# Moving LN apply and the phi clamps to the vector engine, transposing all of x first, and giving the projections two PSUM banks

## The chip, the cores and the metric

The kernel runs on one core of a Trainium2 chip. The metric is the time of one launch in device microseconds. Five engines work side by side, each with its own fixed queue of instructions: PE (matmuls), ACT (activations), DVE (vector), POOL (the general-purpose engine) and SP, which issues DMAs. Results of PE lie in eight PSUM banks of 512 float32 columns each. DVE and ACT read them; POOL does not in this kernel.

## The reference, cut to what matters

One x of 2048 tokens by 448 channels goes through two branches that a gate mixes:

```
g = sigmoid((x * gate_w).sum(-1))
a = A(x)                      # 16 heads of 28, 4 segments of 512 tokens
b = B(x)                      # token-mixing MLP, 2048 -> 1792 -> 2048
out = g * a + (1 - g) * b

A: q, k, v = x @ wq, x @ wk, x @ wv
   phi(t) = where(t > 0, t + 1, exp(t))
   per segment s, M and z starting from 0:
     a_dot = softmax(q k^T * scale + causal mask) v
     a_mem = (phi(q) M) / (phi(q) z + 1e-6)
     o = sigmoid(beta) * a_mem + (1 - sigmoid(beta)) * a_dot
     M += phi(k)^T v ;  z += sum(phi(k))
   return o @ wo
B: h = layernorm(x) over channels
   u = gelu(w1^T h + b1) ; y = w2^T u + b2      # contraction over tokens
```

## The kernel before, in words

**Tiles.** x is held in `xh` as 16 tiles of 128 tokens by 448 channels. `transposes(tc)` (L461 to L485) turns the four tiles of token chunk tc into `xT`: two groups ("halves") of eight 128-column PE transposes (L471), each group into one PSUM bank, and one copy-out per group (L484 on DVE; the very first, L481, on ACT). For each chunk, `do_k` (L499) and `do_q` (L520) make four projection tiles each through `proj_d` (four matmuls of 512 columns, L491); k is copied out by ACT (L503), q by DVE (L524). `do_v` (L539) makes one tile per 128 tokens (four matmuls of 449 columns, L545; the last column is the gate), copied out by ACT (L551, and L554 for the gate's tanh).

**phi.** `do_kphi` (L506) and `do_qphi` (L527) compute phi as max(t, 0) + min(exp(t), 1): the exponential on ACT (L509, L530), the clamp (L511, L532), and one DVE instruction that adds the max (L513, L535). phi of k is then transposed by a DMA that SP issues (L516) from one of two `kphi` buffers. `do_mst(s)` (L557) multiplies the transposed phi(k) of segment s with v (16 matmuls, L564), adds to the running float32 state (L574, L577) and writes the scaled state `mst_sb` (L579).

**Attention.** There are 16 units of one segment and four heads, in order of segment. `scores` (L664) makes three blocks per unit in banks 0 to 3 (L675), takes one exponential over four banks (L684, ACT), and masks the diagonal 128 columns on POOL (L688). `pv_unit` (L692) multiplies with v into bank 4 (L711) and, from unit 4 on, makes the product with the memory state in bank 5 (L697). DVE transposes both (L724, L725), divides (L733 to L736), POOL adds them (L738) and DVE transposes back (L744). `wo_tile` (L750) multiplies a finished 128-token tile with wo (L757) and gates it on ACT (L763); it uses bank 5 too, and for the last tiles banks 0 to 2.

**MLP.** LN needs statistics of each tile (L623, L625, DVE), then four small instructions on POOL for all tiles together (`ln_coef`, L628: L632 to L636, of which L633 is a power), then `ln_apply` (L638), one tensor-scalar with two per-partition scalars per tile, in place on `xh`. `mm1` (L769) makes each of the 14 tiles of u from 16 matmuls of 448 columns, one per token tile (L774), then GELU with three ACT and two DVE instructions (L778 to L789). `mm2` (L793) makes each of 16 output tiles from 14 matmuls (L799), one DVE instruction (L804) and a DMA out. `mlp_next` gives MLP tile i bank 6 + i % 2. Weights of both layers come in 15 loads of 256 columns (`ring_load`, L386) through seven slots, of which three have memory of their own; the fourth and fifth lie on `xT`, the sixth on the padded wq and wk, the seventh on the transposed phi(k), and each of these can be loaded once its first owner is done.

**What sets the order.** Every instruction is declared to a planner (`Sched`, L49) with an engine, the tiles it reads and writes, an estimated cost and a priority. Dependences follow the order of declaration: who writes a bank waits for all who were declared earlier on that bank. `plan` (L113) then plays a greedy list schedule with these costs and freezes each engine's order; on the chip each engine runs its list strictly in order. Lower priority numbers go first: copies-out and small work 0, attention 100 plus the unit, projections, phi and LN around 200, wo 300, MLP1 400, MLP2 500. A DMA is one more such instruction on the queue that issues it.

**Banks.** `next_bank` (L440) hands out `banks_now` (L438) in rotation: all eight for the first chunk, then banks 5, 6, 7 (L828). The rotation counts transposes, projection tiles and the state product alike. In iteration tc of the loop at L830 the order of declaration is transposes(tc), k, q and v of tc, the gate columns, `do_mst(tc - 1)`, then phi of q and k. All of this is declared before attention and MLP. `fn_warm` (L444) runs matmuls on zeros at the start, before x has landed.

Of the kernel before, what the change touches and what calls it, by code (L numbers as in the profile page):

```python
# [5 lines left out]
ACT = mybir.ActivationFunctionType  # L6
ALU = mybir.AluOpType
# [34 lines left out]


ENGINES = ("PE", "ACT", "DVE", "POOL", "SP")
HOP = 70.0
SWITCH = 110.0


class Sched:  # L49
# [11 lines left out]
    def op(self, eng, fn, reads=(), writes=(), name=None, dma=False, out=False, cost=100.0, lat=None, prio=None,  # L61
           mode=None, nbytes=0):
        o = Op()
        o.eng, o.fn, o.name, o.idx = eng, fn, name, len(self.ops)
        o.is_event, o.ev_val, o.knowledge, o.waits = False, None, None, None
        o.cost = cost
        o.lat = (170.0 if eng == "PE" else 0.0) if lat is None else lat
        o.prio = (self.now if prio is None else prio, o.idx)
        o.mode = mode
        o.nbytes = nbytes  # L70
        o.start = o.end = o.pos = None
        if dma:
# [24 lines left out]
        for r in writes:  # L97
            w = r.last_write
            if w is not None:
                (after if r.psum and eng == "PE" and w.evspace == "PE" else need)(w)  # L100
            for rd in r.reads:
                (after if r.psum and eng == "PE" and rd.evspace == "PE" else need)(rd)
        o.deps = list(deps.values())
        o.order = list(order.values())
        for r in reads:
            r.reads.append(o)
        for r in writes:
            r.last_write = o
            r.reads = []
        self.ops.append(o)  # L110
        return o
# [119 lines left out]


def act_cost(n, sbuf=False, ptr=0):
    return n / 1.2 + (115.0 if sbuf else 75.0) + 90.0 * ptr


def dve_cost(n, rate=1.0):
# [1 line left out]


def pool_cost(n):
    return n / 1.2 + 200.0


def build_kernel(nc, X, WQ, WK, WV, WO, BETA, W1, B1, W2, B2, GW, OUT):
# [108 lines left out]

    xv = x2.rearrange("(t p) d -> p t d", p=128)

    def load_x(t0, n):
        op("SP", lambda e: e.dma_start(xh[:, t0 : t0 + n, :], xv[:, t0 : t0 + n, :]),
           writes=R_x[t0 : t0 + n], name=f"ldx{t0}", dma=True, cost=500, nbytes=n * 128 * 896)
# [9 lines left out]
    load_x(4, 4)  # L369
    load_x(8, 4)  # L370
    load_x(12, 4)
# [71 lines left out]

    def fn_warm(e):  # L444
        last = None
        for _ in range(9):
            last = e.matmul(bank(7)[:, 0:512], warm[:, 0:128], warm[:, 0:512], start=True, stop=True,  # L447
                            skip_group_check=True)
# [12 lines left out]
    def transposes(tc):  # L461
        for half in range(2):
            b = next_bank()
            tb = bank(b).bitcast(BF16)

            def fn(e, half=half, tb=tb):
                last = None
                for ti in range(4):
                    for c2 in range(2):
                        c = half * 2 + c2  # L470
                        last = e.matmul(tb[0:CK, c2 * 512 + ti * 128 : c2 * 512 + ti * 128 + 128],  # L471
                                        xh[:, 4 * tc + ti, c * CK : c * CK + CK], ident[:, :], is_transpose=True,
                                        start=True, stop=True, skip_group_check=True)
                return last

            op("PE", fn, reads=R_x[4 * tc : 4 * tc + 4] + [R_ident], writes=[R_bank[b]], name=f"trx{tc}_{half}",
               mode="f", cost=8 * 66, prio=P_PROJ + tc - (50 if tc else 0))
            dst = xT[0:CK, 2 * half : 2 * half + 2, tc * 512 : tc * 512 + 512]
            src = tb[0:CK, :].rearrange("p (c t) -> p c t", c=2)
            if tc == 0 and half == 0:  # L480
                op("ACT", lambda e, dst=dst, src=src: e.activation(dst, src, ACT.Copy), reads=[R_bank[b]],  # L481
                   writes=[R_xT[tc][half]], name=f"xTcp{tc}_{half}", cost=act_cost(1024), prio=P_BASE)
            else:
                op("DVE", lambda e, dst=dst, src=src: e.tensor_copy(dst, src), reads=[R_bank[b]],  # L484
                   writes=[R_xT[tc][half]], name=f"xTcp{tc}_{half}", cost=dve_cost(1024), prio=P_PROJ + tc - 150)  # L485

    def proj_d(w_pad, R_w, hg, tc, b):
        def fn(e):
# [17 lines left out]
    def do_kphi(tc, hg):  # L506
# [1 line left out]
        ks = kT[:, hg, tc * 512 : tc * 512 + 512]  # L508
        op("ACT", lambda e: e.activation(kphi[:, p, :], ks, ACT.Exp), reads=[R_kT[hg][tc]],  # L509
           writes=[R_kphi[p]], name=f"ek{tc}_{hg}", cost=act_cost(512, True), prio=P_PROJ + tc)  # L510
        op("POOL", lambda e: e.tensor_scalar(kphi[:, p, :], kphi[:, p, :], 1.0, 0.0, op0=ALU.min, op1=ALU.max),  # L511
           reads=[R_kphi[p]], writes=[R_kphi[p]], name=f"mk{tc}_{hg}", cost=pool_cost(512), prio=P_PROJ + tc)
        op("DVE", lambda e: e.scalar_tensor_tensor(kphi[:, p, :], ks, 0.0, kphi[:, p, :], op0=ALU.max, op1=ALU.add),  # L513
           reads=[R_kT[hg][tc], R_kphi[p]], writes=[R_kphi[p]], name=f"phk{tc}_{hg}", cost=dve_cost(512),
           prio=P_PROJ + tc)
# [11 lines left out]
    def do_qphi(tc, hg):  # L527
# [1 line left out]
        ph = phq[:, hg, (tc - 1) * 512 : tc * 512]  # L529
        op("ACT", lambda e: e.activation(ph, qs, ACT.Exp), reads=[R_qT[hg][tc]],  # L530
           writes=[R_phq[hg][tc]], name=f"eq{tc}_{hg}", cost=act_cost(512, True), prio=P_PROJ + tc)
        op("POOL", lambda e: e.tensor_scalar(ph, ph, 1.0, 0.0, op0=ALU.min, op1=ALU.max),  # L532
           reads=[R_phq[hg][tc]], writes=[R_phq[hg][tc]], name=f"mq{tc}_{hg}", cost=pool_cost(512),
           prio=P_PROJ + tc)
        op("DVE", lambda e: e.scalar_tensor_tensor(ph, qs, 0.0, ph, op0=ALU.max, op1=ALU.add),  # L535
           reads=[R_qT[hg][tc], R_phq[hg][tc]], writes=[R_phq[hg][tc]], name=f"phq{tc}_{hg}", cost=dve_cost(512),
# [99 lines left out]
        po(lambda e: e.tensor_tensor(nmr[:], vpe[:], rstd[:], op=ALU.mult), [R_vpe, R_rstd], [R_nmr], "nmr")  # L636

    def ln_apply(t):  # L638
        op("POOL", lambda e: e.tensor_scalar(xh[:, t, :], xh[:, t, :], rstd[:, t : t + 1], nmr[:, t : t + 1],  # L639
                                             op0=ALU.mult, op1=ALU.add),  # L640
           reads=[R_x[t], R_rstd, R_nmr], writes=[R_x[t]], name=f"ln{t}", cost=580, prio=P_PROJ - 10)

    def gate_cols(s):
        t4 = slice(4 * s, 4 * s + 4)
# [19 lines left out]
    def scores(n):  # L664
# [21 lines left out]
        for c0 in (0, 384) if f == 1 else (0,):  # L686
            d = pv[:, :, c0 : c0 + 128]
            op("POOL", lambda e, d=d: e.affine_select(d, d, pattern=[[0, 4], [1, 128]], compare_op=ALU.is_ge,  # L688
                                                      fill=0.0, base=0, channel_multiplier=-1),
               reads=[R_P[u % 2][f]], writes=[R_P[u % 2][f]], name=f"mask{n}_{c0}", cost=740, prio=pr)  # L690

    def pv_unit(u):  # L692
        s, hg = unit(u)
# [38 lines left out]
        if s > 0:  # L732
# [3 lines left out]
            dv(lambda e: e.tensor_tensor(t3[1], t3[1], rb[1], op=ALU.mult), [R_tt[tb][1], R_rec[tb]], [R_tt[tb][1]],  # L736
               "om", 650)
            op("POOL", lambda e: e.tensor_tensor(o, t2[:, 0, :], t2[:, 1, :], op=ALU.add), reads=R_tt[tb],  # L738
               writes=[R_ob[tb]], name=f"o{u}", cost=1350, prio=pr)
# [4 lines left out]
        dv(lambda e: e.transpose(oT[:, hg, s * 512 : s * 512 + 512], o), [R_ob[tb]], [R_qT[hg][s]], "ot", 500)  # L744

    def ag(T):
        s, g = divmod(T, 4)
# [174 lines left out]
```

## Time and profile before

| | |
|---|---|
| three runs | 222.96, 223.94, 226.82 us (median 223.94) |
| the profiled execution | 224.56 us, span from first to last instruction 222.8 us |
| mean granted PE clock over the span | 0.954 |
| first scores matmul | 21.05 us |
| first exponential of attention (L684) | 21.64 us |
| first MLP1 matmul (L774) | 85.7 us |
| first MLP2 matmul of the final run (L799) | 177.56 us |
| HBM read and written | 18.13 MB and 1.84 MB |

How to read it: the page gives each engine's busy time over the span; the span in 40 slices, with the clock that PE was granted; the chain of work that ended last, followed back from the last instruction; and groups of equal instructions by line, engine and shape, with busy time, count, mean in ns, and the idle time before them with what ended it. A matmul's row shows its latency, so a back-to-back run is better read from its start and end: 224 matmuls of L799 take 42.39 us. Some matmul records are missing from a trace.

### The profile page before, as it was taken

The page shows a single profiled execution, that of the slowest core. Times are in us where ns is not written, and L with a number is a line of the kernel's source. Part 1 is how long each engine was busy: PE and PEld are TensorE (multiplying, and loading weights), DVE is VectorE, ACT ScalarE, POOL GpSimd, SP SyncE. Part 2 cuts the span into 40 slices and gives each one's busy share as a digit, 9 for nine tenths or more (in the row PEclk, how much of TensorE's full clock was granted, in tenths as well). Part 3 has the DMA queues.
Part 4 walks back from the last instruction along what each step waited for, and adds up shares of the span by engine and source line. Part 5 has one row for each costly group of instructions (what it writes and reads, how often), then busy time and mean ns, then how long its engine had stood idle before and what let it go on. Part 6 is the DMA issues. An engine that isn't in the chain of part 4 may idle for free.

```text
span 222.8 us, 3401 instructions
## 1 busy us (share of the span) xinstructions
PE 194.6 (87%) x1343; PEld 86.7 (39%) x1350; DVE 145.3 (65%) x261; ACT 138.1 (62%) x181; POOL 105.8 (47%) x133
## 2 busy tenths in 40 slices
PE   7599696968866988958879898999999999999994
PEld 2434342423432324312334343434444555555552
DVE  1759895549994497998997957866868142222222
ACT  2264999676995699936999878999975610000000
POOL 8120419999999567966484445455452000000000
PEclk9999999679996799985999999999999999999999
DMA  5999802000101201139640744352355067111111
GB/s 125 297 272 288 206 0 47 4 1 19 29 3 24 47 4 23 24 71 302 175 93 3 188 134 119 79 165 73 95 166 165 3 185 206 41 55 51 41 41 41
DMA packets 42451, 21.75 MB, mean 98 GB/s; under 512 B 7876, under 2 KB 42436, under 8 KB 42436
## 3 DMA queue, kind: packets, MB, share of 16 engines
q1 hardware_dynamic: 41304, 21.13, 35.7%
q10 hardware_dynamic: 1132, 0.41, 1.0%
q8 instruction: 10, 0.16, 0.3%
q14 instruction: 5, 0.04, 0.1%
HBM read 18.13 MB, written 1.84 MB: 90 GB/s over the span
## 4 chain that ended last, share of the span: by engine, by line
PE 52%; DVE 17%; POOL 16%; ACT 12%; issue 2%
PE t L799 19%; PE t L774 11%; PE t L491 7%; ACT t L684 6%; POOL t L639 6%; POOL t L688 5%; PE t L757 4%; PE t L545 3%; PE t L711 2%; DVE t L734 2%; DVE t L736 2%; DVE t L784 2%; PE t L675 2%; PE t L447 2%; DVE t L744 2%
## 5 line engine op out<-in xcount | busy, mean ns | idle before, releaser
L684 ACT ACTIVATE t<-t 128x2048 bf16<-128x2048 f32 (+1 forms) x48 | 77.2, 1608 | 5.4 <-PE t L675 5.3
L688 POOL TENSOR_SCALAR_AFFINE_SELECT t<-t 128x512 bf16<-128x512 bf16 x64 | 47.5, 747 | 39.2 <-ACT t L684 38.1
L774 PE MATMUL t<-t 128*128 128x448 bf16 x224 | 50.6, 359 | 2.4 <-ACT t L781 1.3
L799 PE MATMUL t<-t 128*128 128x448 bf16 x224 | 42.5, 352 | 0.0
L491 PE MATMUL t<-t 112*128 112x512 bf16 x128 | 35.8, 425 | 4.2 <-DVE t L484 2.1
L774 PEld LDWEIGHTS t<-t 128*128 128x128 bf16 x224 | 20.7, 99 | 24.2 <-issue 7.2
L804 DVE SCALAR_TENSOR_TENSOR t<-t 128x448 bf16<-128x448 f32 x16 | 10.9, 684 | 29.0 <-PE t L799 29.0
L799 PEld LDWEIGHTS t<-t 128*128 128x128 bf16 x224 | 21.9, 98 | 20.5 <-DVE t L789 0.2
L738 POOL TENSOR_TENSOR t<-t 128x512 bf16<-128x512 f32 x12 | 16.8, 1401 | 13.3 <-DVE t L736 13.3
L675 PE MATMUL t<-t 28*128 28x512 bf16 (+3 forms) x256 | 17.8, 312 | 5.8 <-ACT t L684 5.7
L491 PEld LDWEIGHTS t<-t 112*128 112x128 bf16 x128 | 12.2, 106 | 21.8 <-issue 6.8
L725 DVE STREAM_TRANSPOSE t<-t 128x512 f32<-128x512 f32 x16 | 11.3, 709 | 11.4 <-PE t L711 11.2
L711 PE MATMUL t<-t 128*32 128x512 bf16 (+3 forms) x256 | 12.7, 322 | 6.9 <-POOL t L688 6.8
L545 PE MATMUL t<-t 112*128 112x449 bf16 x64 | 15.9, 385 | 1.5 <-DVE t L524 1.3
L757 PE MATMUL t<-t 128*128 128x448 bf16 x64 | 15.1, 368 | 1.5 <-DVE t L744 1.3
L784 DVE SCALAR_TENSOR_TENSOR t<-t 128x448 f32<-128x448 f32 x14 | 10.7, 766 | 7.1 <-ACT t L781 6.8
L503 ACT ACTIVATE t<-t 128x512 bf16<-128x512 f32 x16 | 9.6, 605 | 8.9 <-PE t L491 8.9
L639 POOL TENSOR_SCALAR t<-t 128x448 bf16<-128x448 bf16 x16 | 14.7, 927 | 0.5 <-PE t L471 0.5
L744 DVE STREAM_TRANSPOSE t<-t 128x512 bf16<-128x512 bf16 x16 | 11.2, 703 | 4.7 <-POOL t L738 4.6
L675 PEld LDWEIGHTS t<-t 28*128 28x128 bf16 x256 | 5.2, 92 | 22.9 <-ACT t L684 16.3
L511 POOL TENSOR_SCALAR t<-t 128x512 bf16<-128x512 bf16 x12 | 9.2, 768 | 8.1 <-ACT t L509 8.1
L524 DVE CAST t<-t 128x512 bf16<-128x512 f32 x16 | 10.8, 680 | 3.4 <-PE t L491 3.1
(75 smaller groups left out, 230.9 us busy)
## 6 DMA issues: line engine op xcount, KB each, us to landing
t<-in_B_w_dram SPq DMA_DIRECT2D x7, 1024.0 KB, 6.2
t<-in_B_w_dram SPq DMA_DIRECT2D x8, 896.0 KB, 5.2
out_dram<-t SPq DMA_DIRECT2D x16, 112.0 KB, 1.7
t<-in_A_x_dram SPq DMA_DIRECT2D x3, 448.0 KB, 9.0
t<-in_A_x_dram SPq DMA_DIRECT2D x2, 224.0 KB, 5.0
t<-in_A_wk_dram ACTq DMA_DIRECT2D x1, 392.0 KB, 4.5
t<-in_A_wq_dram SPq DMA_DIRECT2D x1, 392.0 KB, 6.8
t<-in_A_wv_dram SPq DMA_DIRECT2D x1, 392.0 KB, 7.8
```

What stands on the lines that cost most here:

```text
L491: last = e.matmul(bank(b)[:, 0:512], w_pad[0:CK, c, hg * 128 : hg * 128 + 128], xT[0:CK, c, tc * 512 : tc * 512 + 512], start=(c == 0), st ...
L545: last = e.matmul(bank(b)[:, 0 : D + 1], xT[0:CK, c, t * 128 : t * 128 + 128], wvx[0:CK, c, :], start=(c == 0), stop=(c == NCT - 1), skip_ ...
L639: op("POOL", lambda e: e.tensor_scalar(xh[:, t, :], xh[:, t, :], rstd[:, t : t + 1], nmr[:, t : t + 1], op0=ALU.mult, op1=ALU.add), reads= ...
L675: last = e.matmul(bank(hl)[:, c0 : c0 + w_], kT[r, hg, s * 512 + j * 128 : s * 512 + j * 128 + 128], qT[r, hg, s * 512 + 128 * j : s * 512 ...
L684: op("ACT", lambda e: e.activation(pv, ps[:, 0:4, 0:w], ACT.Exp, scale=SCALE), reads=R_bank[0:4], writes=[R_P[u % 2][f]], name=f"exp{n}", ...
L688: op("POOL", lambda e, d=d: e.affine_select(d, d, pattern=[[0, 4], [1, 128]], compare_op=ALU.is_ge, fill=0.0, base=0, channel_multiplier=- ...
L711: last = e.matmul(bank(CTX)[32 * hl : 32 * hl + 32, 128 * j : 512], vaug[:, 4 * s + j, 32 * h : 32 * h + 32], pv[:, hl, c0 : c0 + w_], sta ...
L738: op("POOL", lambda e: e.tensor_tensor(o, t2[:, 0, :], t2[:, 1, :], op=ALU.add), reads=R_tt[tb], writes=[R_ob[tb]], name=f"o{u}", cost=135 ...
L744: dv(lambda e: e.transpose(oT[:, hg, s * 512 : s * 512 + 512], o), [R_ob[tb]], [R_qT[hg][s]], "ot", 500)
L757: last = e.matmul(bank(b)[:, 0:D], oT[:, hg, T * 128 : T * 128 + 128], wo_sb[:, hg, :], start=(hg == 0), stop=(hg == NHG - 1), skip_group_ ...
L774: op("PE", lambda e, st=st: e.matmul(bank(b)[:, 0:D], w1c[:, st, f2 * 128 : f2 * 128 + 128], xh[:, st, :], start=(st == 0), stop=(st == NT ...
L799: op("PE", lambda e, ft=ft: e.matmul(bank(b)[:, 0:D], w2c[:, ft, t2_ * 128 : t2_ * 128 + 128], uT[:, ft, :], start=(ft == 0), stop=(ft == ...
```

## The change

- `ln_apply` goes from POOL to DVE, the clamps of phi too (as a min with 1 alone, in place of a min and a max with 0).
- The transposes of chunks 1, 2 and 3 are declared among the v tiles of chunk 0, on the eight-bank rotation, at priority 200. `ln_coef` and `ln_apply` are declared right after the statistics.
- The later projections and state products rotate over banks 5 and 6; MLP1 tiles 0 to 3 all use bank 7, and later tiles alternate as before (tile 4 on 6, tile 5 on 7).
- `do_mst(s)` is declared one iteration later, after the projections of chunk s + 2, and the last one after the loop.
- The warm-up has 18 matmuls in place of 9.
- Tiles 2 and 3 of x are loaded from ACT's queue, wk from SP's queue behind tiles 0 and 1.
- Constants of the planner's cost model are changed: the hop between engines (70 to 80 ns), a delay behind ACT of 95 ns, slightly other costs of ACT, POOL, masks and transposes.

```
-HOP = 70.0
+HOP = 80.0
...
-        o.lat = (170.0 if eng == "PE" else 0.0) if lat is None else lat
+        o.lat = {"PE": 180.0, "ACT": 95.0}.get(eng, 0.0) if lat is None else lat
...
-    load_x(0, 2)
-    load_x(2, 2)
-    op("ACT", lambda e: e.dma_start(wk_nat[0:CK], WK.rearrange("(c p) d -> p c d", p=CK)), writes=R_P[0],
+    load_x("SP", 0, 2)
+    load_x("ACT", 2, 2)
+    op("SP", lambda e: e.dma_start(wk_nat[0:CK], WK.rearrange("(c p) d -> p c d", p=CK)), writes=R_P[0],
...
-        for _ in range(9):
+        for _ in range(18):
             last = e.matmul(bank(7)[:, 0:512], warm[:, 0:128], warm[:, 0:512], start=True, stop=True,
...
-               mode="f", cost=8 * 66, prio=P_PROJ + tc - (50 if tc else 0))
+               mode="f", cost=8 * 66, prio=P_PROJ)
...
-        op("POOL", lambda e: e.tensor_scalar(kphi[:, p, :], kphi[:, p, :], 1.0, 0.0, op0=ALU.min, op1=ALU.max),
-           reads=[R_kphi[p]], writes=[R_kphi[p]], name=f"mk{tc}_{hg}", cost=pool_cost(512), prio=P_PROJ + tc)
+        op("DVE", lambda e: e.tensor_scalar_min(kphi[:, p, :], kphi[:, p, :], 1.0),
+           reads=[R_kphi[p]], writes=[R_kphi[p]], name=f"mk{tc}_{hg}", cost=dve_cost(512, 4), prio=P_PROJ + tc)
...
-        op("POOL", lambda e: e.tensor_scalar(ph, ph, 1.0, 0.0, op0=ALU.min, op1=ALU.max),
-           reads=[R_phq[hg][tc]], writes=[R_phq[hg][tc]], name=f"mq{tc}_{hg}", cost=pool_cost(512),
+        op("DVE", lambda e: e.tensor_scalar_min(ph, ph, 1.0),
+           reads=[R_phq[hg][tc]], writes=[R_phq[hg][tc]], name=f"mq{tc}_{hg}", cost=dve_cost(512, 4),
...
-        op("POOL", lambda e: e.tensor_scalar(xh[:, t, :], xh[:, t, :], rstd[:, t : t + 1], nmr[:, t : t + 1],
-                                             op0=ALU.mult, op1=ALU.add),
-           reads=[R_x[t], R_rstd, R_nmr], writes=[R_x[t]], name=f"ln{t}", cost=580, prio=P_PROJ - 10)
+        op("DVE", lambda e: e.tensor_scalar(xh[:, t, :], xh[:, t, :], rstd[:, t : t + 1], nmr[:, t : t + 1],
+                                            op0=ALU.mult, op1=ALU.add),
+           reads=[R_x[t], R_rstd, R_nmr], writes=[R_x[t]], name=f"ln{t}", cost=dve_cost(448, 4), prio=P_PROJ - 10)
...
     do_small()
+    transposes(1)
     for t in range(4):
         do_v(t)
+        if t == 1:
+            transposes(2)
+    transposes(3)
     for t in range(NT):
         ln_stats(t)
+    ln_coef()
+    for t in range(NT):
+        ln_apply(t)
     load_wo()
...
-    banks_now[0] = [5, 6, 7]
+    banks_now[0] = [5, 6]
     gate_cols(0)
     for tc in (1, 2, 3):
-        transposes(tc)
...
         gate_cols(tc)
-        do_mst(tc - 1)
+        if tc > 1:
+            do_mst(tc - 2)
         for hg in range(NHG):
             do_qphi(tc, hg)
             if tc < 3:
                 do_kphi(tc, hg)
-    ln_coef()
-    for t in range(NT):
-        ln_apply(t)
+    do_mst(2)
     for _ in range(4):
         ring_load()
+    NB7 = 4
...
-        f_(a, 6 + i % 2)
+        f_(a, 7 if i < NB7 else 6 + i % 2)
```

More of the change, by code (lines that the diff above doesn't have):

```diff
@@ L233, in act_cost @@
 def act_cost(n, sbuf=False, ptr=0):
-    return n / 1.2 + (115.0 if sbuf else 75.0) + 90.0 * ptr
+    return n / 1.2 + (100.0 if sbuf else 80.0) + 90.0 * ptr
 def dve_cost(n, rate=1.0):
@@ L241, in pool_cost @@
 def pool_cost(n):
-    return n / 1.2 + 200.0
+    return n / 1.2 + 320.0
 def build_kernel(nc, X, WQ, WK, WV, WO, BETA, W1, B1, W2, B2, GW, OUT):
@@ L355, in build_kernel, with load_x @@
     xv = x2.rearrange("(t p) d -> p t d", p=128)
-    def load_x(t0, n):
-        op("SP", lambda e: e.dma_start(xh[:, t0 : t0 + n, :], xv[:, t0 : t0 + n, :]),
+    def load_x(eng, t0, n):
+        op(eng, lambda e: e.dma_start(xh[:, t0 : t0 + n, :], xv[:, t0 : t0 + n, :]),
            writes=R_x[t0 : t0 + n], name=f"ldx{t0}", dma=True, cost=500, nbytes=n * 128 * 896)
-    load_x(0, 2)
-    load_x(2, 2)
-    op("ACT", lambda e: e.dma_start(wk_nat[0:CK], WK.rearrange("(c p) d -> p c d", p=CK)), writes=R_P[0],
+    load_x("SP", 0, 2)
+    load_x("ACT", 2, 2)
+    op("SP", lambda e: e.dma_start(wk_nat[0:CK], WK.rearrange("(c p) d -> p c d", p=CK)), writes=R_P[0],
        name="ldwk", dma=True, cost=500, nbytes=401408)
@@ L368, in build_kernel @@
        name="ldwv", dma=True, cost=500, nbytes=401408)
-    load_x(4, 4)
-    load_x(8, 4)
-    load_x(12, 4)
+    for t0 in (4, 8, 12):
+        load_x("SP", t0, 4)
     op("ACT", lambda e: e.dma_start(wvx[0:CK, :, D : D + 1], GW.rearrange("(c p o) -> p c o", p=CK, o=1),
@@ L484, in transposes @@
                 op("DVE", lambda e, dst=dst, src=src: e.tensor_copy(dst, src), reads=[R_bank[b]],
-                   writes=[R_xT[tc][half]], name=f"xTcp{tc}_{half}", cost=dve_cost(1024), prio=P_PROJ + tc - 150)
+                   writes=[R_xT[tc][half]], name=f"xTcp{tc}_{half}", cost=dve_cost(1024, 2), prio=P_PROJ + tc - 150)
     def proj_d(w_pad, R_w, hg, tc, b):
@@ L689, in scores @@
                                                       fill=0.0, base=0, channel_multiplier=-1),
-               reads=[R_P[u % 2][f]], writes=[R_P[u % 2][f]], name=f"mask{n}_{c0}", cost=740, prio=pr)
+               reads=[R_P[u % 2][f]], writes=[R_P[u % 2][f]], name=f"mask{n}_{c0}", cost=750, prio=pr)
     def pv_unit(u):
@@ L738, in pv_unit @@
             op("POOL", lambda e: e.tensor_tensor(o, t2[:, 0, :], t2[:, 1, :], op=ALU.add), reads=R_tt[tb],
-               writes=[R_ob[tb]], name=f"o{u}", cost=1350, prio=pr)
+               writes=[R_ob[tb]], name=f"o{u}", cost=1400, prio=pr)
         else:
@@ L743, in pv_unit @@
                [R_tt[tb][0], R_rec[tb], R_omcol], [R_ob[tb]], "oa", 650)
-        dv(lambda e: e.transpose(oT[:, hg, s * 512 : s * 512 + 512], o), [R_ob[tb]], [R_qT[hg][s]], "ot", 500)
+        dv(lambda e: e.transpose(oT[:, hg, s * 512 : s * 512 + 512], o), [R_ob[tb]], [R_qT[hg][s]], "ot", 700)
     def ag(T):
```

## The prediction

> **What bounds the kernel now.** I read the page first: engine totals, clock row, and the chain that ended last.
>
> ```profile
> PE 194.6 (87%) x1343; PEld 86.7 (39%) x1350; DVE 145.3 (65%) x261; ACT 138.1 (62%) x181; POOL 105.8 (47%) x133
> PEclk9999999679996799985999999999999999999999
> PE 52%; DVE 17%; POOL 16%; ACT 12%; issue 2%
> ```
>
> No engine is full over the span, and POOL, the least busy, owns 16% of the chain. So the stages have different limits. I cut the span where the chain changes hands: first scores (21.05), POOL's run (33.37 to 68.84), the first read of unit 4's memory product (84.87), the last projection's consumer (102.84), the first MLP2 matmul (177.56).
>
> ```profile
> core 0: us, PE busy (x) PEld busy (x) DVE busy (x) ACT busy (x) POOL busy (x), PEclk, DMA share, GB/s
> 0.00:21.05 21.05, 17.19 (x72) 7.52 (x73) 12.31 (x50) 7.27 (x13) 6.97 (x15) 1.00 0.97 243
> 21.05:33.37 12.32, 10.17 (x92) 4.72 (x92) 10.87 (x28) 11.55 (x14) 3.39 (x5) 1.00 0.50 122
> 33.37:68.84 35.47, 25.81 (x215) 11.09 (x214) 26.16 (x41) 28.10 (x40) 34.45 (x43) 0.89 0.10 20
> 68.84:84.87 16.03, 14.75 (x100) 5.33 (x101) 10.11 (x17) 12.28 (x19) 11.36 (x16) 0.81 0.13 26
> 84.87:102.84 17.97, 14.36 (x117) 6.26 (x119) 17.76 (x24) 14.14 (x19) 14.13 (x15) 0.89 0.30 74
> 102.84:177.56 74.72, 70.00 (x531) 30.05 (x534) 55.90 (x87) 63.02 (x76) 35.51 (x42) 0.98 0.44 120
> 177.56:222.80 45.24, 42.37 (x224) 21.69 (x222) 12.20 (x18) 1.73 (x3) 0.00 (x0) 1.00 0.27 82
> 21.05:177.56 156.51, 135.08 (x1051) 57.45 (x1058) 120.80 (x194) 129.09 (x165) 98.84 (x118) 0.93 0.32 83
> ```
>
> The columns are the stretch, its length and each engine's busy time. From 33.37 POOL is busy 34.45 of 35.47 us while ACT has 28.10 and DVE 26.16. From 84.87 DVE is full (17.76 of 17.97). From 102.84 it is PE (70.00 of 74.72), and after 177.56 MLP2 alone. The pieces of the chain say what POOL was doing:
>
> ```profile
> 34.69 2.93 POOL t L633
> ...
> 39.40 3.22 POOL t L639 x4
> ...
> 43.21 2.79 POOL t L639 x4
> ...
> 51.27 1.60 POOL t L511 x2
> 52.87 2.17 POOL t L532 x3
> ...
> 64.75 3.45 POOL t L639
> ...
> 70.64 4.85 PE t L491 x12
> ...
> 177.56 42.39 PE t L799 x224
> ```
>
> LN apply (L639) and clamps (L511, L532) stand ahead of the masks and of the phi tiles. Behind those the projections queue, because the memory-state product of a segment holds a place in the rotation of their three banks and waits for phi. Unit 4 cannot start its memory product until bank 5 is through with projections:
>
> ```profile
> 83.67 0.94 PE L545 MATMUL t<-t 112*128 112x449 bf16 x4 [0.21 <-ACT t L554]
> ...
> 84.87 0.72 DVE L724 STREAM_TRANSPOSE t<-t 128x512 f32<-128x512 f32 x1 [1.04 <-PE t L545]
> ```
>
> MLP1 shares banks 6 and 7 with them and so starts as late:
>
> ```profile
> L774 PE MATMUL t<-t x224: 349/353/581, 85.7 to 177.2; 128*128 128x448 bf16 x112
> ```
>
> So from 102.84 PE carries nearly all of MLP1, although it had gaps before: 33.37 to 68.84 holds 9.7 us without a matmul, and a granted clock of 0.89 on what ran.
>
> **The change, part by part.** The rows that price it:
>
> ```profile
> L639 POOL TENSOR_SCALAR t<-t 128x448 bf16<-128x448 bf16 x16 | 14.7, 927 | 0.5 <-PE t L471 0.5
> L532 POOL TENSOR_SCALAR t<-t 128x512 bf16<-128x512 bf16 x12 | 9.5, 803 | 2.4 <-ACT t L530 2.4
> L511 POOL TENSOR_SCALAR t<-t 128x512 bf16<-128x512 bf16 x12 | 9.2, 768 | 8.1 <-ACT t L509 8.1
> L457 DVE COPY t<-t 112x1792 bf16<-112x1792 bf16 x1 | 0.6, 619 | 0.0
> L645 DVE TENSOR_SCALAR t<-t x4: 154/340/596, 36.3 to 103.5; 128x4 f32<-128x4 f32 x4
> L513 DVE SCALAR_TENSOR_TENSOR t<-t 128x512 bf16<-128x512 bf16 x12 | 11.4, 960 | 0.0
> L684 ACT ACTIVATE t<-t 128x2048 bf16<-128x2048 f32 x32 | 60.4, 1889 | 5.0 <-PE t L675 4.9
> L503 ACT ACTIVATE t<-t 128x512 bf16<-128x512 f32 x16 | 9.6, 605 | 8.9 <-PE t L491 8.9
> L784 DVE SCALAR_TENSOR_TENSOR t<-t 128x448 f32<-128x448 f32 x14 | 10.7, 766 | 7.1 <-ACT t L781 6.8
> L789 DVE SCALAR_TENSOR_TENSOR t<-t 128x448 bf16<-128x448 f32 x14 | 9.7, 693 | 4.0 <-ACT t L787 4.0
> ```
>
> POOL loses 14.7 + 9.5 + 9.2 = 33.4 us. DVE gains 40 instructions of a form that the trace lacks. From below: a bf16 copy of 1792 elements takes 0.619 us and the smallest tensor-scalar 0.154, so 0.26 ns an element; 448 elements are then 0.27 us and 512 are 0.29, in all 16 x 0.27 + 24 x 0.29 = 11.3 us. From above: the two-tensor op on 512 elements at 0.96 makes 38 us. I take 11.3 plus waiting. The waiting shows in L645: four-element work takes 0.154 at best and 0.596 at worst, with POOL's own instructions running beside it. Half the excess of its median, 0.09 on 40, is 3.7 us; the whole, 0.19, is 7.4. Against it, POOL's departed 33.4 us stop delaying L513 and its like, whose mean I expect to fall by about 0.2 of 0.96, some 5 us over the 24 phi tiles. DVE net: about +10 us on 120.8 over the long stretch.
>
> The Trainium skill's SBUF — State Buffer (Who interferes with whom) says that a VectorE op in a two-port mode and a GpSimd op shut each other out for the whole instruction, the later one blocking; L645's 0.596 agrees. By that rule at its worst each of the 40 would wait out one mask, and DVE would gain far more than by the copy row alone; this speaks against the change.
>
> A new wait: the LN applies now stand in DVE's fixed queue behind POOL's power (L633, 2.93 us), which the planner costs at 250 ns. It will queue the first of them up to 2.7 us too early, and behind them the copies of q and the attention's DVE work. Between 0 and 2.7; I take 1.0, since ACT has scores to go on with.
>
> Head. Rows of the same chain:
>
> ```profile
> 1.24 4.02 PE t L447 x9
> ...
> 7.01 1.94 PE t L471 x16
> ...
> 9.81 3.57 PE t L491 x8
> ...
> 13.52 5.29 PE t L491 x24
> ...
> 60.45 0.58 PE t L471 x8
> ```
>
> The warm-up runs at 0.45 us a matmul, and so do the first 8 projection matmuls; the next 24 take 0.22. Eighteen warm-ups end between 7.2 (second nine at 0.22) and 9.3 (all at 0.45), so the transposes at 7.01 start 0.2 to 2.3 late. If the pace then stays full, 16 transposes save about 0.8 and 8 projections 1.8. Net between 2.4 earlier and 2.3 later (slow pace anyway); I take 1 earlier.
>
> The Trainium skill's TensorE: Matmul & The Clock Gate (Part 1) has the array at half rate until a window of about 3.4 us was busy. The full pace from 13.5, 3.6 us after the projections began, agrees; by the rule eighteen would do it before the transposes, and the sum would take the full 2.4.
>
> The six later transpose groups (0.58 each, 3.5 us) now stand before the first scores, since they use banks 3 and 4 (their copies, L484, too), with the fourth v tile (0.9). 21.05 - 1 + 3.5 + 0.9 is 24.5, less half a microsecond of overlap: scores at 24.0, bounds 22 and 27. It is a loss for ACT, whose exponentials start there, repaid on PE later. The load of wk moves behind the first x load on SP and one x load goes to ACT's queue ahead of the small ones: half a microsecond of issue, hidden since the padded wk is not used before 9.81; uncovered it costs that 0.5.
>
> Banks. The state product of segment s now comes a round later, so projections no longer wait for phi; that removes the queue behind POOL. In exchange 39 tiles share two banks. A cycle of a bank is 4 matmuls (0.94 in L545's row, 1.04 with 512 columns), the copy-out (L503, 0.6) and a part of an exponential (L684, 1.89) in front of it on ACT: with half of one, 2.6 us, or 1.3 a tile, so 39 x 1.3 = 51 us, ending near 75 instead of 84.87. The new cost constants move only the planned order; no instruction changes with them, and I price them at 0 within the bounds of ACT's share below.
>
> MLP1. LN can be done by about 45, and groups 0 to 3 and 5 use bank 7, free of projections: 5 x 16 x 0.189 (42.39/224) = 15.1 us of PE leave the full stretch after 102.84 for the gaps before. They bring 5 x (0.766 + 0.693) = 7.3 us of DVE early.
>
> The sum. PE and POOL are then no longer full; ACT's work is unchanged and sets the end of the attention. ACT had 129.1 in 156.5 us, 82.5%; its best stretch (21.05 to 33.37, no POOL trouble) reached 94%. I take 90%: above the middle, because both things that held it, POOL early and PE late, are cut by more than ACT's idle time there. DVE would have 131 in 143 us, which it can do (99% in one stretch). So 24.0 + (129.1 - 0.7 for the earlier v copy-out)/0.90 = 24.0 + 142.7, + 1.0 for the wait = 167.7 for the first MLP2 matmul, + 45.24 = 212.9 of span. The profiled execution took 224.56 for 222.8, so + 1.76: **214.7 us**, against its 224.56; the median of the runs is 0.6 lower (223.94), which is within the noise of the forecast. Only what differs by over 2% (219.5 and 228.4) can be told from no change here.
>
> **The rivals.**
>
> First, better: ACT reaches 94%, 24.0 + 136.6 + 47.0 = 207.6, and below this MLP2 starts under the last two units: some 5 us of its matmuls, 202. For it: the stretch that did reach 94%. Against: DVE would then be at 96%.
>
> Second, no change: DVE takes POOL's place. Early (21.05 to 102.84) it had 64.9 of 81.8 us; 11.3, 7.4 of waiting and 7.3 of GELU make 90.9, less 4 for the transposes' copies and 5 for relief, 82, with no room to shrink. ACT's share then stays at 82.5 to 86%, and the end at 24.0 + 150 to 156 + 47.0 = 221 to 227; 224 in the middle. For it: DVE is full from 84.87 to 102.84. Against: later DVE has slack (55.9 of 74.7) and work can slide there. The Trainium skill's SBUF — State Buffer (Who interferes with whom), by its blocking rule above, gives this rival more weight.
>
> Third, slower: two banks starve the projections. If each copy-out waits for a whole 1.89 us exponential, a cycle is 3.5 plus handovers, 1.85 a tile, and 39 tiles end at 24 + 72 = 96; the ACT work left after unit 4's start (14.1 + 63.0, less 5 x 3 GELU instructions of about L503's 0.6 moved ahead of it, 68) at 80 to 84% is 81 to 85, so 96 + 83 + 47 + the wait of 1 = 227, to 231 with the planner's misplaced waits. It decides from about 1.8 us a tile on. Its price: 229. For it: copy-outs queue on an in-order ACT. Against: they have first priority, and half of a wait is the mean.
>
> **How the numbers follow.** The forecast has 0.55 (own range 207.6 to 219, that is 94% to 87%), the better case 0.16, no change 0.19, slower 0.10. For 8 in 10 the range takes in most of no change and half of the better case: 203 to 225. Faster by over 2%: 0.55 + 0.16 = 0.71; within 2%: 0.19 and a little of the slower case, 0.20; slower by over 2%: 0.09.
>
> **What would show it.** Right: POOL near 72 us in all; first scores near 24; first MLP1 matmul before 55; unit 4's L724 near 75; the three state products no longer ahead of projections; ACT at 88 to 92% from scores to MLP2, which starts near 168; the granted clock near full from 45 on. LN and clamps each 0.25 to 0.4 on DVE. Wrong: DVE full from 30 to 100 with ACT waiting on it (second rival); PE waiting on copy-outs of banks 5 and 6, unit 4 after 90 (third); the first projections still at 0.45 (head).

## The result, and the profile after

The changed kernel takes 210.13 us (median of four runs, 208.89 to 211.06) where the kernel before, run beside it, takes 223.45. The ratio is 0.941, with an interval from 0.9335 to 0.9484: it is faster by 5 to 7%. The forecast was 214.7 us. Medians are over all executions of a kernel, while ratios leave out single slow ones at a lower granted clock, such as 219.71 us of the kernel with six tiles on bank 7 and 213.21 us of the one with nine warm-ups.

The page of the changed kernel, the rows that answer to those quoted of before:

```profile
PE 189.4 (91%) x1359; PEld 84.8 (41%) x1359; DVE 153.4 (73%) x301; ACT 136.7 (65%) x181; POOL 73.7 (35%) x93
PEclk9999999999999799969999999999999999999999
PE 46%; DVE 40%; ACT 7%; POOL 3%; issue 2%
```

POOL has gone from 16% of the chain to 3%, and DVE from 17% to 40%. The granted clock has two short dips where it had three long ones. Now the stages: columns are the stretch, its length and the busy time of PE, PE's weight loads, DVE, ACT and POOL. The cuts are the first scores (23.52), the first LN apply (35.37), the first read of unit 4's memory product (81.83), and the first long run of MLP2 (160).

```profile
0.00:23.52 23.52, 20.87 (x136) 11.03 (x137) 16.25 (x59) 8.18 (x17) 5.30 (x13) 1.00 0.98 252
23.52:35.37 11.85, 10.90 (x84) 4.32 (x84) 11.16 (x29) 11.34 (x14) 6.72 (x9) 1.00 0.29 71
35.37:81.83 46.46, 40.70 (x319) 17.08 (x318) 44.59 (x92) 41.00 (x64) 14.96 (x20) 0.96 0.25 57
81.83:118.50 36.67, 30.40 (x237) 12.28 (x239) 34.09 (x51) 29.04 (x34) 19.58 (x21) 0.95 0.51 134
118.50:160.00 41.50, 40.62 (x332) 17.01 (x332) 30.06 (x48) 39.99 (x47) 22.14 (x25) 1.00 0.36 102
160.00:176.20 16.20, 16.20 (x108) 7.89 (x107) 9.02 (x15) 6.39 (x8) 4.98 (x6) 1.00 0.38 109
176.20:208.80 32.60, 29.70 (x158) 15.16 (x155) 8.21 (x12) 0.73 (x2) 0.00 (x0) 1.00 0.13 43
23.52:160.00 136.48, 122.62 (x964) 50.69 (x964) 119.91 (x217) 121.37 (x156) 63.40 (x74) 0.97 0.36 93
```

The reader is to see three things. From 35 to 118 DVE is at 95% (44.59 + 34.09 of 83.13 us), where POOL was the full one before. From 118 to 160 PE and ACT are both nearly full. And from 156.6 on MLP2 runs among the last units, from 160 in long runs; before, it began only when PE had nothing else left. The rows of the chain that show it:

```profile
1.24 6.12 PE t L446 x18
...
35.37 5.96 DVE t L639 x16
...
84.74 1.29 DVE t L511
...
160.00 0.67 PE t L799 x3
...
173.18 3.03 PE t L757 x16
176.20 29.71 PE t L799 x157
```

Only 157 of MLP2's 224 matmuls are left when the last wo tiles (L757) are done; 67 of them, 12.7 us at 0.189 each, lie under the end of the attention. The attention itself ends no earlier than before. The lines of wo, its last matmuls, and of MLP2, first in the kernel before and then in the changed one:

```profile
L757 PE MATMUL t<-t x64: 350/353/581, 87.5 to 174.4; 128*128 128x448 bf16 x64
L799 PE MATMUL t<-t x224: 352/352/353, 177.4 to 219.6; 128*128 128x448 bf16 x112
```

```profile
L757 PE MATMUL t<-t x64: 352/353/364, 82.5 to 175.8; 128*128 128x448 bf16 x64
L799 PE MATMUL t<-t x224: 352/353/364, 156.6 to 205.5; 128*128 128x448 bf16 x112
```

The last wo matmul starts at 175.8 and not at 174.4, and the last exponential (L684) at 163.8 and not at 162.4. Before, the last matmul of MLP1 (177.2) came after the attention's, and MLP2 had to wait for it. What makes room for MLP2 now is MLP1, which starts at 35.9 and not at 85.7 and is through at 156.4. Here is the work of MLP1's line alone up to 102.84, the time at which the last projection's consumer stood before the change; the columns are PE and weight loads. First the kernel before, then the changed one:

```profile
0.00:102.84 102.84, 2.94 (x12) 1.38 (x13) 0.91 0.36 88
```

```profile
0.00:102.84 102.84, 19.51 (x76) 7.09 (x76) 0.97 0.51 128
```

And in the changed kernel the durations (least, median, most, in ns) and first and last start of MLP1's line and of the memory product's first reader:

```profile
L774 PE MATMUL t<-t x224: 349/353/582, 35.9 to 156.4; 128*128 128x448 bf16 x112
L724 DVE STREAM_TRANSPOSE t<-t x12: 668/704/717, 81.8 to 157.7; 128x512 f32<-128x512 f32 x12
```

64 more matmuls at 0.189 us are 12.1 us of PE work carried forward. The time fell by 13.3 us (223.45 - 210.13).

A part of this can be the clock's. The granted clock over the span rose from 0.954 to 0.984, and PE's busy time fell from 194.6 to 189.4 us although the warm-up has nine matmuls more. No run fills the gaps at an unchanged clock, so the two are not told apart. The clock alone does not set the order of the kernels: one of those below is faster than the changed kernel, 207.26 us, at 0.967.

### The profile page after: what moved, and what is told of

It is laid out like the page before. It is cut to its first block, busy times and chain, and to the rows that moved or that the text cites. A ratio compares the mean times of both kernels' runs of the same rounds, so it can differ in the third digit from the quotient of the medians.

```text
span 208.8 us, 3428 instructions
## 1 busy us (share of the span) xinstructions
PE 189.4 (91%) x1359; PEld 84.8 (41%) x1359; DVE 153.4 (73%) x301; ACT 136.7 (65%) x181; POOL 73.7 (35%) x93
## 4 chain that ended last, share of the span: by engine, by line
PE 46%; DVE 40%; ACT 7%; POOL 3%; issue 2%
PE t L799 20%; PE t L491 6%; PE t L757 5%; PE t L774 4%; ACT t L684 4%; DVE t L513 3%; DVE t L734 3%; DVE t L725 3%; DVE t L535 3%; PE t L711 3%; DVE t L744 3%; PE t L446 3%; DVE t L639 3%; DVE t L736 3%; DVE t L724 2%; DVE t L511 2%
## 5 line engine op out<-in xcount | busy, mean ns | idle before, releaser
L684 ACT ACTIVATE t<-t 128x2048 bf16<-128x2048 f32 (+1 forms) x48 | 77.6, 1616 | 5.3 <-PE t L675 5.0
L688 POOL TENSOR_SCALAR_AFFINE_SELECT t<-t 128x512 bf16<-128x512 bf16 x64 | 47.6, 750 | 70.6 <-ACT t L684 69.3
L774 PE MATMUL t<-t 128*128 128x448 bf16 x224 | 52.6, 360 | 1.7 <-ACT t L781 1.7
L799 PE MATMUL t<-t 128*128 128x448 bf16 x224 | 43.4, 353 | 0.0
L491 PE MATMUL t<-t 112*128 112x512 bf16 x128 | 31.8, 389 | 6.9 <-DVE t L524 5.0
L774 PEld LDWEIGHTS t<-t 128*128 128x128 bf16 x224 | 20.4, 99 | 24.7 <-issue 8.1
L799 PEld LDWEIGHTS t<-t 128*128 128x128 bf16 x224 | 21.6, 98 | 20.3 <-issue 0.5
L738 POOL TENSOR_TENSOR t<-t 128x512 bf16<-128x512 f32 x12 | 17.5, 1456 | 26.5 <-DVE t L736 26.5
L491 PEld LDWEIGHTS t<-t 112*128 112x128 bf16 x128 | 11.1, 99 | 22.0 <-DVE t L524 5.8
L763 ACT ACTIVATE t<-t 128x448 bf16<-128x448 f32 x16 | 11.7, 731 | 9.7 <-PE t L757 9.6
L757 PE MATMUL t<-t 128*128 128x448 bf16 x64 | 14.3, 355 | 4.0 <-DVE t L724 3.8
L545 PE MATMUL t<-t 112*128 112x449 bf16 x64 | 14.5, 361 | 0.0
L551 ACT ACTIVATE t<-t 128x448 bf16<-128x448 f32 x16 | 8.7, 562 | 7.4 <-PE t L545 7.4
L675 PEld LDWEIGHTS t<-t 28*128 28x128 bf16 x256 | 5.2, 92 | 19.3 <-ACT t L684 12.4
L623 DVE BATCH_NORM_STATS2 t<-t 128x6 f32<-128x448 bf16 x16 | 9.5, 597 | 2.6 <-DMA t<-in_A_x_dram 2.6
```

The source lines that it names most:

```text
L491: last = e.matmul(bank(b)[:, 0:512], w_pad[0:CK, c, hg * 128 : hg * 128 + 128], xT[0:CK, c, tc * 512 : tc * 512 + 512], start=(c == 0), st ...
L545: last = e.matmul(bank(b)[:, 0 : D + 1], xT[0:CK, c, t * 128 : t * 128 + 128], wvx[0:CK, c, :], start=(c == 0), stop=(c == NCT - 1), skip_ ...
L675: last = e.matmul(bank(hl)[:, c0 : c0 + w_], kT[r, hg, s * 512 + j * 128 : s * 512 + j * 128 + 128], qT[r, hg, s * 512 + 128 * j : s * 512 ...
L684: op("ACT", lambda e: e.activation(pv, ps[:, 0:4, 0:w], ACT.Exp, scale=SCALE), reads=R_bank[0:4], writes=[R_P[u % 2][f]], name=f"exp{n}", ...
L757: last = e.matmul(bank(b)[:, 0:D], oT[:, hg, T * 128 : T * 128 + 128], wo_sb[:, hg, :], start=(hg == 0), stop=(hg == NHG - 1), skip_group_ ...
L774: op("PE", lambda e, st=st: e.matmul(bank(b)[:, 0:D], w1c[:, st, f2 * 128 : f2 * 128 + 128], xh[:, st, :], start=(st == 0), stop=(st == NT ...
```

## The experiments

Each kernel ran beside the kernel before; ratios are to it, with their intervals. Theory A is the one of the prediction, that MLP1 work fills PE's gaps early. Theory B is that a cleared POOL queue is the gain.

**LN and clamps back on POOL.** In the changed kernel:

```
-        op("DVE", lambda e: e.tensor_scalar(xh[:, t, :], xh[:, t, :], rstd[:, t : t + 1], nmr[:, t : t + 1],
+        op("POOL", lambda e: e.tensor_scalar(xh[:, t, :], xh[:, t, :], rstd[:, t : t + 1], nmr[:, t : t + 1],
...
-        op("DVE", lambda e: e.tensor_scalar_min(kphi[:, p, :], kphi[:, p, :], 1.0),
+        op("POOL", lambda e: e.tensor_scalar(kphi[:, p, :], kphi[:, p, :], 1.0, 0.0, op0=ALU.min, op1=ALU.max),
```

and the same for the clamp of q.

> The changed kernel with LN apply and both clamps on POOL again, everything else changed. Theory A (the gain is MLP1 work that can run before the last projection, because LN is early and bank 7 is free of projections): LN still comes early enough on POOL, MLP1 starts some 10 to 20 us later than at 35.9 but long before 85, DVE is relieved of 18.7 us; 208 to 214 us. Theory B (the gain is that POOL's queue of masks is cleared of 33 us): nearly all of the gain is lost, 219 to 224 us.

Measured: 215.06 us, 0.9605 (0.9572 to 0.9638). MLP1 ran 74 matmuls before 102.84, nearly as many as in the changed kernel, the first at 36.6 and not 10 to 20 us later as theory A had it, and yet 5 us are lost. It falls between the two theories: of the gain of 5.9%, about two thirds stand without the move to DVE and a third does not.

**Three banks for the projections again.**

```
-    banks_now[0] = [5, 6]
+    banks_now[0] = [5, 6, 7]
...
-        f_(a, 7 if i < NB7 else 6 + i % 2)
+        f_(a, 6 + i % 2)
```

> The changed kernel with the projections on banks 5, 6, 7 again and MLP1 alternating between 6 and 7. Theory A: MLP1 cannot start before the last projection on bank 6 or 7, near 75 to 80, some 12 us of PE work go back to the full stretch at the end; 218 to 223 us. Theory B: POOL stays clear, a third bank only helps the projections; 207 to 212 us.

Measured: 217.21 us, 0.9711 (0.9672 to 0.9751). The projections now end earlier (first read of unit 4's memory product at 74.0 in place of 81.8) and still half of the gain is gone. MLP1's work up to 102.84 in that kernel, then the first and last start of its line and of unit 4's reader, say where:

```profile
0.00:102.84 102.84, 7.15 (x33) 2.94 (x34) 0.90 0.45 110
```

```profile
L774 PE MATMUL t<-t x224: 349/353/555, 88.9 to 166.6; 128*128 128x448 bf16 x112
L724 DVE STREAM_TRANSPOSE t<-t x12: 668/708/717, 74.0 to 159.0; 128x512 f32<-128x512 f32 x12
```

MLP1 starts at 88.9 although LN's last apply (L639) starts at 44.9; the bank kept it back. The projections are not what holds the bank so long, for their last matmul starts at 69.8. By the rotation the second state product has bank 6, that of the first MLP1 tile, and MLP1 starts when the DVE instruction that reads it, L577, is done:

```profile
88.89 1.86 PE L774 MATMUL t<-t 128*128 128x448 bf16 x9 [0.55 <-DVE t L577]
```

That is theory A, at 217.2 just under its 218, but with the state product in the place of the last projection.

**Only the clamps on POOL**, LN on DVE: the second half of the first diff.

> The changed kernel with only the clamps on POOL again (24 instructions, 12.7 us off DVE), LN apply on DVE. If DVE is the bound of the changed kernel from 35 to 118 us, as its 95% busy there suggests: 203 to 208 us, POOL near 92 us busy. If the phi chain on POOL behind the masks is what held the kernel before: 212 to 217 us.

Measured: 211.3 us, 0.9429 (0.9388 to 0.947), no different from the changed kernel's 0.941. Both readings missed. DVE's busy time fell by only 5.0 us (148.4 of 153.4), since other lines on it got longer: L789 by 1.4 us in all, L784 by 1.2, L535 by 1.1. That POOL's clamps beside them did this is argued.

**The move to DVE alone**, on the kernel before: LN and clamps on DVE, nothing else.

> The kernel before with LN apply and both clamps on DVE and nothing else. Theory A: MLP1 still waits for the projections on its banks; at most a few us from POOL, 218 to 225 us. Theory B: most of the gain is here, 209 to 214 us.

Measured: 219.34 us, 0.9801 (0.9749 to 0.9853). A third of the gain, the same third that the first run lost, and inside theory A's range. MLP1 ran 32 matmuls before 102.84.

**The state products at their former place.**

```
-        if tc > 1:
-            do_mst(tc - 2)
+        do_mst(tc - 1)
...
-    do_mst(2)
```

> The changed kernel with each state product declared at its former place, an iteration earlier, on the rotation of two banks. Theory A (MLP1 in the gaps carries most of the gain, the projections only a part): the state product of segment 0 now stands ahead of chunk 2's projections and waits for phi of k, unit 4 later by up to 5 us; 210 to 214 us. Theory C (the projections freed from phi carry the gain): 216 us or more.

Measured: 206.53 us, 0.9238 (0.9205 to 0.927). It is faster than the changed kernel, which no theory had. MLP1's work in this kernel, and then the lines of unit 4's memory product and of the clamp of k:

```profile
0.00:102.84 102.84, 21.62 (x87) 7.72 (x87) 0.98 0.55 133
```

```profile
L724 DVE STREAM_TRANSPOSE t<-t x12: 666/688/709, 92.8 to 150.7; 128x512 f32<-128x512 f32 x12
L511 DVE TENSOR_SCALAR t<-t x12: 251/285/324, 31.2 to 83.4; 128x512 bf16<-128x512 bf16 x12
```

Unit 4 reads its memory product at 92.8, 11 us later than in the changed kernel and 8 later than before the change, in the faster kernel. So that point does not set the end. What differs is that phi of k is through at 83.4, before the units with memory begin, while in the changed kernel it goes on to 98.9 among them and waits beside POOL's adds; there the same line reads:

```profile
L511 DVE TENSOR_SCALAR t<-t x12: 250/306/1365, 31.0 to 98.9; 128x512 bf16<-128x512 bf16 x12
```

ACT gets 34.2 us of work into 81.83 to 118.50 in the faster kernel and 29.0 in the changed one, and the last exponential starts at 158.2 and not at 163.8. That phi's place is the cause of it is argued from these rows and was not tried by itself.

**Transposes at their former place.** The transposes of chunks 1 to 3 go back into the loop with their former priority, LN stays declared where the change put it.

```
-    transposes(1)
...
-    transposes(3)
...
     for tc in (1, 2, 3):
+        transposes(tc)
```

> The changed kernel with the transposes of chunks 1 to 3 at their former place in the loop and at their former priority. LN overwrites x in place, so its last tiles wait for the last transposes, which stand behind the projections of chunk 2 on banks 5 and 6. Theory A: MLP1 starts only near 60 to 70 and most of the gain of MLP1 goes; 215 to 221 us, with the first scores 2 to 3 us earlier. Theory B (a clear POOL queue is enough): 209 to 212 us.

Measured: 207.26 us, 0.9273 (0.9234 to 0.9313). The expectation rests on a wrong premise: LN is declared first here, so it does not wait for the transposes, and the projections of chunks 1 to 3 are taken from normalized x, so this kernel computes something else. The run does not tell theory A from B. It shows that MLP1, started at 31.7 and with 85 matmuls before 102.84, goes with a short time once more, although unit 4 comes at 97.8. Its first scores come at 19.3, 4.2 us earlier than in the changed kernel, which is a gain of its own.

**LN after the last transposes**, to mend that: transposes in the loop as above, and LN's coefficients and apply declared behind the loop.

> The changed kernel with the transposes of chunks 1 to 3 back in the loop and LN's coefficients and apply declared after the loop, so that LN waits for the last transposes as before the change; bank 7 stays with MLP1, the clamps and LN stay on DVE. Theory A (early LN and a free bank together carry MLP1 forward): first MLP1 matmul near 60 to 70, at most half of the 76 matmuls before 102.84, 213 to 219 us. Rival (the free bank alone is enough): 206 to 212 us.

Measured: 213.72 us, 0.9514 (0.9425 to 0.9603). MLP1's line up to 102.84:

```profile
0.00:102.84 102.84, 12.61 (x50) 4.73 (x51) 0.98 0.52 124
```

50 matmuls in place of 76, and the median is up by 3.6 us; theory A's side, but the interval overlaps that of the changed kernel, so its size is uncertain. The first scores come at 19.5 here, 4 us earlier, so the late LN may cost more than the difference shows. The first MLP1 matmuls ran at 32.1, on the tiles that were ready, and 50 is more than the half that was expected, so those parts of the expectation were wrong.

**Nine warm-ups** in the changed kernel (`range(18)` to `range(9)`).

> The changed kernel with 9 warm-up matmuls. If the long warm-up is what put the transposes and the first projections at full pace: 8 projection matmuls at 0.43 in place of 0.22 and slower transposes, first scores at 25 to 26 in place of 23.5, 211 to 213 us. If something else did: no difference, 209.5 to 210.5 us.

Measured: 210.62 us, 0.940 (0.9349 to 0.9451): no difference. The timeline of this kernel's start:

```profile
1.24 4.02 PE L446 MATMUL t<-t 128*128 128x512 bf16 x9 [1.24 <-DVE t L605]
...
5.05 1.78 PE L471 MATMUL t<-t 128*112 128x128 bf16 x16
...
8.44 2.75 PE L491 MATMUL t<-t 112*128 112x512 bf16 x12 [1.60 <-DVE t L452]
```

The transposes start at 5.05 straight after the warm-up; before, they started at 7.01 after 1.75 us of idle PE. That the second load of x has landed by then because it stands on ACT's queue is argued. They run at slow pace, but the projections after them at 0.23 us each, as with 18 warm-ups. So the full pace of the first projections needs no long warm-up here. That it is the shorter idle time which gives it is read from these rows; the load's queue was not undone by itself. The kernel with the cost constants alone (below) has nine warm-ups too, up to 5.26, and then:

```profile
6.23 1.07 PE L471 MATMUL t<-t 128*112 128x128 bf16 x16 [0.97 <-issue]
11.03 3.57 PE L491 MATMUL t<-t 112*128 112x512 bf16 x8 [3.73 <-DVE t L484]
```

After 0.97 us of idle PE its transposes run at full pace, and after 3.73 us more its projections are slow again, at 0.45 us each. So the idle time ahead of the projections counts as well. Each of these is one execution. The eighteen hold the transposes back to 7.4, and with nine the first scores come at 22.3 in place of 23.5.

**The cost constants alone**, on the kernel before.

> The kernel before with nothing but the new constants of the planner's cost model; not an instruction differs, only the order. My price was zero: 222 to 226 us. Rival: the better fitting order is a good part of the gain, 217 to 220 us.

Measured: 220.06 us, 0.9833 (0.9792 to 0.9875). Not one instruction differs, and the new order is worth 3.6 us. My price of zero was wrong; the rival's range ended at 220, just below.

**No clamps.** The changed kernel without the two clamp instructions.

> The changed kernel with both clamps left out, so that phi is exp(t) + max(t, 0) without the min with 1; 24 instructions and 12.7 us of busy time less on DVE, nothing in their place. If DVE is the bound from 35 to 118 us (95% busy): 201 to 206 us. If DVE is only as full as ACT and PE and the order of PE's work decides: 207 to 211 us.

Measured: 207.41 us, 0.9239 (0.9169 to 0.9309). The clamps are 12.7 us of busy time on the engine that is at 95% for 83 us (DVE's total falls by 9.4), and leaving them out brings 2.7 us by the medians, 3.8 by the ratios. From 35.37 to 118.50 PE and ACT are now at 89% and DVE at 88%. So DVE holds the changed kernel a little, and PE and ACT behind it at once.

**Two variants of the faster kernel** with the early state products. With the clamps on POOL:

> The fastest so far (the changed kernel with the state products at their former place, 206.5 us) with the clamps on POOL as well, where 33 us became free. If DVE's load holds that kernel: 202 to 205.5 us. If the clamps cost on POOL what they free on DVE, as they did in the changed kernel: 206 to 209 us.

Measured: 211.21 us, 0.9409 (0.9342 to 0.9476), 4.7 us slower than without and above both readings: the clamps' move to DVE is worth that here. With six MLP1 tiles on bank 7 (`NB7 = 6`):

> The fastest so far with MLP1 tiles 0 to 5 all on bank 7 (as many as have weights in memory of their own) in place of 0 to 3 and 5. Theory A, a dose more: tile 4 no longer waits for bank 6; more than 87 MLP1 matmuls before 102.84 and 203 to 206 us. If the gaps are already filled: no difference, 206 to 207.5 us.

Measured: 206.61 us, 0.9204 (0.9098 to 0.931), no difference, with 88 matmuls before 102.84: the gaps were filled already.

All kernels in order of MLP1's matmuls before 102.84 us:

| kernel | matmuls | median us |
|---|---|---|
| before | 12 | 223.45 |
| costs alone | 19 | 220.06 |
| move alone | 32 | 219.34 |
| three banks | 33 | 217.21 |
| LN after transposes | 50 | 213.72 |
| clamps on POOL | 66 | 211.30 |
| LN and clamps on POOL | 74 | 215.06 |
| changed | 76 | 210.13 |
| nine warm-ups | 78 | 210.62 |
| early state products, clamps on POOL | 80 | 211.21 |
| no clamps | 84 | 207.41 |
| transposes late, from normalized x | 85 | 207.26 |
| early state products | 87 | 206.53 |
| early state products, six on bank 7 | 88 | 206.61 |

From the first row to the last 76 matmuls and 16.8 us, 0.22 a matmul where one costs 0.189. So a matmul carried forward goes with about its own time on PE. The two rows out of line, by 3 to 5 us, have clamps on POOL, but so has a third that is in line; what the two lose it by was not settled. The table is a correlation; what was shown by taking it away is the bank (three banks). The shares found above, a half for the bank, a third for the move to DVE, 1.7% for the constants on the kernel before, overlap and are not to be added.

## Why the prediction was right, point by point

The number and the range were right, and so was the main idea, MLP1 in PE's early gaps. The path of the sum was not: it had the attention end sooner, and that did not happen. Two errors offset each other, so the closeness of 214.7 to 210.13 is in part luck.

**MLP1 early: right in kind, smaller by a fifth.** Predicted 15.1 us of PE work moved; 12.1 were, by the count above. Taking the bank away (three banks) costs half of the gain, with LN early all the same; that is shown. It started at 35.9, well before 55. POOL came to 73.7 us, near the 72 of the forecast.

**Head: right in the sum, wrong in a cause.** Scores were put at 24.0 and came at 23.52. The warm-up ended at 7.4, inside 7.2 to 9.3. But the gain was credited to the warm-up, and nine do as well; the x load on ACT's queue, priced as a hidden half microsecond of issue, comes with the earlier transposes. What the Trainium skill's TensorE: Matmul & The Clock Gate (Part 1) says of a busy window was read as asking for eighteen; the rows of nine agree with it too, if the transposes that follow at once count for the window.

**DVE's load: right in the net, the parts off.** +10 us were predicted and 145.3 became 153.4, +8.1. The 40 instructions take 18.7 us, not 15, and the rest of DVE's work fell by 10.6, not 5. LN costs 0.38 undisturbed where the copy row gave 0.27, and 0.45 in the mean; clamps cost 0.25 where it gave 0.29, and with waiting 0.58 (k) and 0.48 (q) in the mean. The lines of LN and of the clamp of q:

```profile
L639 DVE TENSOR_SCALAR t<-t x16: 382/390/779, 35.3 to 40.9; 128x448 bf16<-128x448 bf16 x16
L532 DVE TENSOR_SCALAR t<-t x12: 251/288/1360, 48.3 to 106.2; 128x512 bf16<-128x512 bf16 x12
```

In return the instructions that follow the clamps got faster, as expected; their mean was 0.91 (L535) and 0.96 (L513), and is now 0.80 and 0.77:

```profile
L535 DVE SCALAR_TENSOR_TENSOR t<-t 128x512 bf16<-128x512 bf16 x12 | 9.6, 804 | 0.3
L513 DVE SCALAR_TENSOR_TENSOR t<-t 128x512 bf16<-128x512 bf16 x12 | 9.2, 770 | 0.3
```

**The wait for the power on POOL: not there.** 1.0 us was put down. LN's coefficients were done at 34.99 and DVE began LN at 35.29, straight from other work.

**Banks and state products: wrong.** "projections no longer wait for phi; that removes the queue behind POOL" was counted as a gain, with unit 4 near 75. It came at 81.8, and undoing just this is 1.8% faster (0.9238 against 0.941). The step failed at its premise, that an earlier memory product of unit 4 is a gain: in two fast kernels it stands at 92.8 and 97.8. My cycle of two banks was near: in the 55 us from 23.5 to 78.4 all but two of the 39 tiles were made, 1.5 a tile against 1.3, far from the 1.8 of the slower rival; the second state product starts at 78.4 and the third at 109.2.

**Cost constants: wrong.** Priced at zero, they are worth 3.6 us by themselves on the kernel before.

**The clock: near full, as forecast.** It is 0.96 from 35.37 to 81.83, 0.95 up to 118.50 and 1.00 after that; the three stages from 33.37 to 102.84 had 0.89, 0.81 and 0.89 before.

**ACT's share and the end of the attention: wrong.** The sum let ACT set the end: 128.4 us of work at 90% from the first scores, so that all but MLP2 is done at 167.7. Up to 160 ACT's share is 121.37 of 136.48, 89%. But the last wo tiles end at 176.20, and up to there it is 84%:

```profile
23.52:176.20 152.68, 138.82 (x1069) 58.58 (x1069) 128.93 (x232) 127.76 (x163) 68.38 (x80) 0.98 0.36 95
```

That is the share of the second rival, no change (82.5 to 86%), and its end of the attention too (24.0 + 150 to 156, so 174 to 180). The step that failed is the reading of before: MLP2 waited at 177.4 for MLP1's last matmul, not for ACT, whose last exponential started at 162.4. So moving MLP1 did not have to shorten the attention to help. Why ACT stays at 84% was not settled; DVE has a part in it, since without the clamps the last exponential starts at 159.8 in place of 163.8.

**Where MLP2 stands: the error on the other side.** The forecast had all of MLP2 follow the attention. 12.7 us of it run under the attention's end, where the first rival had some 5. The two errors offset each other: the attention ends 8.5 us late (176.2 for 167.7), MLP2 has 12.7 us less to do then, and the span is 4.1 us below the forecast (208.8 for 212.9). The second rival had the attention right and this overlap not at all; its sign, DVE full from 30 to 118, is there, but no more than 2.7 to 3.8 us hang on the clamps' 12.7.

## What to carry to other kernels

A filler on the matmul engine is only as early as its buffer: look first for the bank it shares with work of a higher rank, then for what its input waits for. Before counting on a shorter stage, look what the next stage really waits for: here it was the filler, not the attention. When one engine is at 95% and two others near 85% beside it, taking work off the fullest brought a fraction of that work here; count what can start earlier instead. Try each part of a change that reorders work on its own, since the constants of a planner alone moved this kernel by 1.7% and one part of a gainful change cost 1.8%.

## What was not expected of the hardware

The clamp takes 0.25 us alone on DVE and up to 1.36 when it starts beside POOL's float32 add. In the changed kernel's timeline it ends 0.14 us after that add does:

```profile
98.57 1.59 POOL L738 TENSOR_TENSOR t<-t 128x512 bf16<-128x512 f32 x1 [0.63 <-DVE t L736]
98.94 1.36 DVE L511 TENSOR_SCALAR t<-t 128x512 bf16<-128x512 bf16 x1
```

The prediction's bound of one mask (L688, 0.75 us in the mean) for such a wait was too small, 1.1 us here, because it did not think of the add. The Trainium skill's SBUF — State Buffer (Who interferes with whom) has a two-port VectorE op and a GpSimd op shut each other out, the later one blocking until the first is done; these two rows agree. LN apply, with two per-partition scalars, takes 0.38 us on 448 elements where the clamp, with a constant, takes 0.25 on 512.
